# The product with v of a window of rows: all six pairs of heads in one run of matmuls

## The chip, the cores and the metric

The kernel runs on one core of one Trainium2 chip. The metric is device time in microseconds (us), as the median of the runs of one kernel. Engines are named as in the profile: PE is TensorE (PEld its weight loads), DVE VectorE, ACT ScalarE, POOL GpSimd, SP the engine that issues the DMAs.

## The reference

Attention that mixes its heads twice, then two feed-forward blocks. B, H, S, D = 2, 12, 448, 64; the blocks have 896 tokens of 768, with 1536 and 2048 inner columns. All is float32; the weights of the blocks are float64 on input.

```
scores = einsum('bhij,hg->bgij', q @ k.T / sqrt(D), w_pre)
attn   = exp(scores - max(scores)); attn = attn / (sum(attn) + 1e-9)
x      = einsum('bhij,hg->bgij', attn, w_post) @ v      # tokens x 768
xn     = x / sqrt(mean(x * x) + 1e-6) * rms_g
x2     = (silu(xn @ w_gate) * (xn @ w_val)) @ w_out
out    = elu(x2 @ w_in) @ w_out2
```

## The kernel before

The kernel has an attention stage, up to about 293 us, and then products with the weights. The change lies in the attention, so this section keeps to it.

**Scores and groups.** For each batch and head, q and k are transposed on PE (`k_turn`, `q_turn`), multiplied in chunks of 112 rows (`scores`, L407 and L408), copied by ACT (L418) and stored to device memory with (row, head) order (L419). They come back two groups at a time (`load_group`, L440). A group is ten rows, each with its twelve heads: 120 partitions. A batch has 45 groups, the last of eight rows. A group goes through: split into two parts on ACT and POOL (L468, L469; every other group takes the unsplit float32), premix on PE (L476, or L479 to L481), maximum on DVE (L488), exponential on ACT (L496), reciprocal (L511), high and low float16 parts (L524 or L526, and L533), postmix on PE with twelve small matmuls (L554), and a copy by ACT into the tile `at` (L566), which then holds key position on the partitions and (chunk, head, row) along them.

**Windows.** `at` collects the groups of a window: six or seven groups, 48 to 70 rows, seven windows a batch, fourteen in all (`WGS`, L539). When a window's last group is in, `window(b, w)` puts pieces of work into the queue `wq`: the product with v, `av(kk)` for pair kk of heads. One `av` is 16 records on PE (four chunks, two heads, two passes of float32), 64 columns each, the two heads on the two halves of the partitions of one PSUM tile `psv_t` (L590). The last of these pieces also puts the list `chain` into the queue `cq`: squares (DVE L596, then POOL L603 to L606, or ACT L601 for the last two windows), nothing, mean (PE L612), root (DVE, POOL L623), nothing, diagonal (DVE L627), spread (PE L631), normed (DVE L634), high (ACT L640) and low (DVE L643), one piece a step. They leave the normed tokens in `xh` and `xl`. The last window of the first batch then also issues the loads of the second batch's v (L314).

**The order of the work** is written out by hand, in a loop over steps t (from L749). The engines take their instructions in the order in which they are issued. Step t issues, by engine:

- ACT: copies that follow the last step's matmuls; the copy to `at` of group t - 4; split of group t + 3; exponential of group t; high part of group t - 1
- DVE: sum of t - 1, maximum of t, reciprocal of t - 1, low part of t - 2, then what follows the last step's transposes
- PE: premix of t + 1, postmix of t - 3, then 1.4 to 1.5 pieces of scores or transposes a step (later pieces that convert weights, on ACT and DVE), then one piece of each chain in `cq`, then one piece of `wq` (two from t = 90 on)

Premix, scores, transposes, mean and spread share five PSUM buffers (`psa`, L66); a buffer comes free when ACT or DVE has read it. The postmix has two of its own, `psv_t` one, `at` two.

At the end of the attention `first_gate` gives twelve triples of matmuls of the gated block (L197 to L199), which need only the first batch's tokens; `fill` puts them between the last pieces, one a step.

```
        for _ in range(2 if t >= n else 1):
            if wq:
                wq.pop(0)()
        ...
    for _ in range(GAP):
        step_chains()
        fill(1)
    while wq:
        wq.pop(0)()
    while cq:
        step_chains()
        fill(END)
```

Of the kernel before, what the change touches and what calls it, by code (L numbers as in the profile page):

```python
# [21 lines left out]
def block_kernel(  # L22
# [32 lines left out]
    SIGN = -0x80000000  # L55
    # a float64's upper word read as a float32, times REBASE: its exponent three bits
    # to the right of a float32's; F32_MAX is then the largest float32
    REBASE = 2.0**-112
# [12 lines left out]
    def split(h, l, x, h_eng="act"):  # L71
        """x = h + l, each part exact in float32r."""
        if h_eng == "act":
            nc.scalar.activation(out=h, in_=x, func=ACTF.Copy)
        else:
            nc.vector.tensor_copy(out=h, in_=x)
        nc.vector.tensor_tensor(out=l, in0=x, in1=h.bitcast(F32), op=ALU.subtract)

    ctx.enter_context(tc.manual_schedule())

# [1 line left out]
    ident = const.tile([P, P], F32, name="ident")  # L82
# [6 lines left out]
    nc.vector.memset(mhalf, -0.5)  # L89
    # w_pre and w_post once per row of a group, on the diagonal blocks  # L90
    setup = wpool.tile([P, KD * P], F32, tag="w32", name="setup", bufs=1)
# [30 lines left out]
    def mixing():  # L122
        """Pieces that make the matrices that mix the heads."""
        selr, cmax, rcm, m2p = slot(H, GI, H), slot(P, H), slot(P, H), slot(GP, H, GI)
        a1 = m1.rearrange("p i g -> p (i g)")
        a2 = m2.rearrange("p i g -> p (i g)")
        rep = {}

        def select():
            nc.vector.tensor_copy(out=selr, in_=ident[:H, :H].unsqueeze(1).to_broadcast([H, GI, H]))  # L130
            nc.vector.tensor_reduce(
                out=cmax, in_=wpb.rearrange("p (h g) -> p g h", h=H), axis=AXX, op=ALU.max,
                apply_absolute_value=True,
            )
            nc.vector.tensor_scalar_max(cmax, cmax, 1e-30)

        def repeat():
            rep[0] = ps_a()
            nc.tensor.matmul(
                out=rep[0][:GP, :2 * H], lhsT=selr.rearrange("p i h -> p (i h)"),  # L140
                rhs=wpp.rearrange("p t h -> p (t h)"), start=True, stop=True,
            )
            nc.vector.reciprocal(out=rcm, in_=cmax)

        def copies():
            for t, m in enumerate((m1, m2)):
                nc.vector.tensor_copy(
                    out=m, in_=rep[0][:GP, t * H:(t + 1) * H].unsqueeze(1).to_broadcast([GP, GI, H])
                )

        def blocks():
            for m in (m1, m2):
                nc.gpsimd.affine_select(
                    out=m, in_=m, pattern=[[-H, GI], [0, H]], compare_op=ALU.is_ge, fill=0.0, base=0,
                    channel_multiplier=1,
                )
                nc.gpsimd.affine_select(
                    out=m, in_=m, pattern=[[H, GI], [0, H]], compare_op=ALU.is_ge, fill=0.0, base=H - 1,
                    channel_multiplier=-1,
                )  # L160
            # what the postmix leaves to be multiplied, for head 2 k + half on the partitions' halves
            for s in range(2):
                nc.vector.tensor_scalar_mul(
                    vsc[s * D:(s + 1) * D], cmax.rearrange("p (k s) -> p s k", s=2)[s * D:(s + 1) * D, s], BACK
                )

        def pre():
            # premix matrix, with the scores' scale
            nc.vector.tensor_scalar_mul(a1, a1, 1.0 / float(D) ** 0.5)
            nc.vector.tensor_copy(out=m1f, in_=a1)  # L170
            nc.vector.tensor_copy(out=m1h, in_=a1)
            nc.vector.tensor_tensor(out=m1l, in0=a1, in1=m1h.bitcast(F32), op=ALU.subtract)

        def post():
            # postmix matrix: columns of w_post over their maximum, in (head, row) order
            nc.vector.tensor_tensor(
                out=m2, in0=m2, in1=rcm[:GP].unsqueeze(1).to_broadcast([GP, GI, H]), op=ALU.mult
            )
            nc.vector.tensor_scalar_mul(m2p, m2.rearrange("p i g -> p g i"), W_UP)
            nc.vector.tensor_copy(out=m2h, in_=m2p)  # L180
            nc.vector.tensor_tensor(out=m2l, in0=m2p, in1=m2h, op=ALU.subtract)

        return [select, repeat, copies, blocks, None, pre, post]

    # normed tokens, later the first block's output: [d, token]
    xh = xpool.tile([P, KD, NT], F32R, tag="xh", name="xh")
# [3 lines left out]

# [1 line left out]
    HALF = [slice(b * S, (b + 1) * S) for b in range(B)]  # L192

    def gemm(ps, wh, wl, xh_, xl_, nk, first=True, last=True):
        """ps = w.T @ x in three passes of split operands."""
        for kk in range(nk):
            nc.tensor.matmul(out=ps, lhsT=wh(kk), rhs=xh_(kk), start=(first and kk == 0), stop=False)  # L197
            nc.tensor.matmul(out=ps, lhsT=wh(kk), rhs=xl_(kk), start=False, stop=False)  # L198
            nc.tensor.matmul(out=ps, lhsT=wl(kk), rhs=xh_(kk), start=False, stop=(last and kk == nk - 1))  # L199
# [9 lines left out]
    def convert(u):  # L209
        """Pieces that turn a block of float64 weights into float32r parts h + l."""  # L210
        raw, (_, _, nk, nf, scale) = raws[u], units[u]
# [50 lines left out]

    # the weights' blocks in the order of their use, loaded and converted ahead of it
    NH = DM // 2
    units = []
# [7 lines left out]
    raws, ready, begun = [], {}, [0]  # L273
# [14 lines left out]
    def first_gate(j):  # L288
        """The first columns of gate or val for the first batch, a matmul triple at a time."""
        hf = HALF[0]  # L290
# [12 lines left out]
    def attention(actx):  # L303
# [14 lines left out]
        def load_qk(b, h):  # L318
            """q, and k twice side by side."""
            qt = ap.tile([CP, NCH, D], F32, tag="qt", name="qt", bufs=2)  # L320
# [6 lines left out]
        def load_first():  # L327
            """The first heads' q and k at once, in room that is not yet in use."""
            n_at = NCH * H * WMAX
# [22 lines left out]
        def parts_of(b, h):  # L352
            """Room for a head's parts, some of it where the weights will be."""
            if (b, h) not in par:
# [11 lines left out]
        def q_split(b, h):  # L366
            # both parts side by side, so that they come out one above the other
            qt, _ = qk_sb[b, h]
# [5 lines left out]
        def k_turn(b, h):  # L374
            # twice, under both parts of q
            _, kt = qk_sb.pop((b, h))
# [44 lines left out]

        # what follows from the matmuls of the last step
        on_act, on_dve = [], []
# [5 lines left out]

# [1 line left out]
        LG = 2  # L431
# [24 lines left out]
        def whole(b, g):  # L456
            """Groups whose premix takes float32 as it is; the others' takes parts."""
            i = b * NG + g
            return i % WHOLE == 1 and not PARTS[0] <= i < PARTS[1]
# [77 lines left out]

        # windows of groups, for the product with v
        WGS = [[0, 7, 14, 21, 27, 33, 39, NG], [0, 7, 14, 21, 28, 34, 40, NG]]  # L539
# [30 lines left out]
        def window(b, w):  # L570
            """The work after a window's last group, in pieces."""
            t0 = WGS[b][w] * GI
# [85 lines left out]

            return [lambda k0=k0, k1=k1: some(k0, k1) for k0, k1 in ((0, 2), (2, 3), (3, 4), (4, 5), (5, 6))]

# [1 line left out]
        heads = [(b, h) for b in range(B) for h in range(H)]  # L662
        EARLY, FAST, RATE, LATE = 4, 1.5, 1.4, 1.4

        def turn(i):
            """Pieces that leave head i ready for its products."""

# [68 lines left out]
        conv_now = []  # L736
        # the last groups' tail runs beside the next product's first matmuls
        gates = []
# [75 lines left out]
    def run(u, mm, stages):  # L814
        """A unit's matmuls, with the later units' conversion and the earlier one's outputs beside them."""
        load_to(u + 4)
# [13 lines left out]

# [1 line left out]
    uh = big.tile([P, KF, NT], F32R, tag="bh", name="uh", padded_shape=[P, KF2, NT])  # L832
# [71 lines left out]

# [1 line left out]
    gh = big.tile([P, KF2, NT], F32R, tag="bh", name="gh")  # L906
    gl = big.tile([P, KF2, NT], F32R, tag="bl", name="gl")

    def elu(pss, fc):
        # max(-relu(1 - exp(h)), h)  # L910
        t = {}
# [24 lines left out]

# [1 line left out]
    NTT = NT // P  # L938
# [71 lines left out]
```

## Time and profile before

| | |
|---|---|
| median of 3 runs | 788.56 us (787.6 to 790.57) |
| span of the profiled execution, which is the time that the page gives for it | 787.3 us |
| busy in the span: PE, DVE, ACT, POOL | 759.4, 550.6, 445.6, 114.4 us |
| mean granted PE clock | 0.990 |
| product with v (L590), all of it | 1344 records, 55.7 us busy |

The span runs from the first to the last instruction of one profiled execution; the median is 1.3 us longer. Matmuls overlap, so their times are best read from start to start. "Idle before <-releaser" in a row is the time that the engine stood still before the instruction, and what ended it. The granted clock is a share of 2.4 GHz.

### The profile page before, as it was taken

The numbers are of one execution on the slowest core, as the hardware profiler recorded it, in microseconds if no ns is written. First come the engines' busy times: TensorE is split into PE (matmuls) and PEld (weight loads), VectorE is DVE, ScalarE is ACT, GpSimd is POOL, SyncE is SP. The second block draws the span as 40 slices with busy tenths as digits, with TensorE's granted clock in tenths as the row PEclk, the third lists the DMA queues.
The fourth block names the chain that finished last, engine by engine and source line by source line (L and its number), as shares of the span: only waits on it lengthen the run. The fifth ranks groups of instructions, "written<-read, shape, count | busy, mean of one in ns | idle before, by whom it ended". The sixth has DMA issues, their size and how long they took to land.

```text
span 787.3 us, 14708 instructions
## 1 busy us (share of the span) xinstructions
PE 759.4 (96%) x5655; PEld 673.1 (85%) x5655; DVE 550.6 (70%) x1135; ACT 445.6 (57%) x952; POOL 114.4 (15%) x141
## 2 busy tenths in 40 slices
PE   6779999999998999999999999999999999999997
PEld 5557778777776779999999999999999999999997
DVE  6356999665789938887877865652898887553651
ACT  7679888887987925654544433231576566221320
POOL 4212565333443400000000000000000000000000
PEclk9899999999998999999999999999999999999999
DMA  7798665668783303343332333231444343433512
GB/s 205 222 280 252 168 154 140 178 173 236 217 230 78 104 2 121 122 132 108 121 112 94 116 121 106 95 121 41 121 132 120 109 122 100 111 111 111 155 47 70
DMA packets 90249, 105.42 MB, mean 134 GB/s; under 512 B 16004, under 2 KB 86084, under 8 KB 90180
## 3 DMA queue, kind: packets, MB, share of 16 engines
q1 hardware_dynamic: 90180, 104.49, 46.0%
q8 instruction: 44, 0.72, 0.4%
q14 instruction: 25, 0.20, 0.1%
HBM read 82.46 MB, written 22.02 MB: 133 GB/s over the span
## 4 chain that ended last, share of the span: by engine, by line
PE 83%; DVE 7%; DMA 5%; ACT 2%; issue 1%; SPq 1%; POOL 1%; ACTq 0%; POOLq 0%
PE psa_t L197 13%; PE psa_t L198 13%; PE psa_t L199 13%; PE psv_t L590 5%; PE pst_t L554 4%; PE psf_t L198 4%; PE psf_t L199 4%; PE psf_t L197 4%; PE psa_t L966 3%; PE psa_t L964 3%; PE psa_t L965 3%; DMA s_d<-st 3%; PE psa_t L476 3%; DMA sg<-s_d 2%; PE psa_t L407 2%; DVE el L533 1%
## 5 line engine op out<-in xcount | busy, mean ns | idle before, releaser
L554 PEld LDWEIGHTS <-eh 120*112 120x112 f16 x720 | 66.8, 131 | 27.2 <-issue 21.8
L240 ACT ACTIVATE whl<-w 128x768 fp32r<-128x768 f32 x44 | 37.1, 844 | 86.0 <-PE psf_t L966 28.5
L244 ACT ACTIVATE whl<-w,g_sb 128x128 fp32r<-128x128 f32 x144 | 45.0, 393 | 64.1 <-PE psa_t L199 25.6
L219 ACT ACTIVATE w<-raw 128x768 f32<-128x768 f32 x68 | 62.5, 919 | 30.5 <-DVE whl L251 23.6
L469 POOL TENSOR_TENSOR sl<-sg,sh 120x448 fp32r<-120x448 f32 (+1 forms) x45 | 54.5, 1211 | 116.2 <-ACT sh L468 111.6
L251 DVE TENSOR_TENSOR whl<-w,whl 128x768 fp32r<-128x768 f32 x44 | 42.2, 958 | 41.1 <-ACT whl L240 40.0
L198 PE MATMUL psa_t<-x2l,whl 128*128 128x448 f32 x192 | 70.1, 365 | 0.0
L199 PE MATMUL psa_t<-x2h,whl 128*128 128x448 f32 x192 | 70.1, 365 | 0.0
L197 PE MATMUL psa_t<-x2h,whl 128*128 128x448 f32 x192 | 70.1, 365 | 0.0
L233 DVE SCALAR_TENSOR_TENSOR w<-w,raw 128x768 int32<-128x768 int32 x68 | 65.2, 958 | 2.3
L554 PE MATMUL pst_t<-m2h,eh 120*112 120x120 f16 x360 | 63.0, 217 | 2.7 <-ACT at L566 2.6
L227 DVE SCALAR_TENSOR_TENSOR raw<-raw 128x768 int32<-128x768 int32 x68 | 64.8, 953 | 0.0
L554 PE MATMUL pst_t<-m2h,el 120*112 120x120 f16 x360 | 63.1, 218 | 1.7 <-DVE el L533 1.7
L496 ACT ACTIVATE e<-psa_t,nmax 120x448 f32<-120x448 f32 (+1 forms) x90 | 58.0, 645 | 11.4 <-DVE rs L511 10.4
L533 DVE SCALAR_TENSOR_TENSOR el<-e,rs,eh 120x448 f16<-120x448 f32 (+1 forms) x90 | 64.0, 711 | 0.3 <-ACT eh L524 0.3
L554 PE MATMUL pst_t<-m2l,eh 120*112 120x120 f16 x360 | 63.0, 218 | 0.0
L488 DVE TENSOR_REDUCE nmax<-psa_t 120x1 f32<-120x448 f32 (+1 forms) x90 | 55.2, 613 | 8.4 <-PE psa_t L481 8.3
L197 PE MATMUL psa_t<-xh,whl 128*128 128x448 f32 x150 | 55.7, 372 | 1.0 <-ACT xh L640 1.0
L590 PE MATMUL psv_t<-at,vs 112*64 112x70 f32 (+3 forms) x1344 | 55.7, 230 | 0.0
L590 PEld LDWEIGHTS psv_t<-at,vs 112*64 112x64 f32 x1344 | 46.5, 139 | 9.9 <-issue 7.0
L198 PE MATMUL psa_t<-xl,whl 128*128 128x448 f32 x150 | 54.9, 366 | 0.0
L199 PE MATMUL psa_t<-xh,whl 128*128 128x448 f32 x150 | 54.8, 365 | 0.0
(167 smaller groups left out, 2059.2 us busy)
## 6 DMA issues: line engine op xcount, KB each, us to landing
raw<-in_moe_w_out_dram SPq DMA_DIRECT2D x28, 768.0 KB, 4.5
sg<-s_d SPq DMA_DIRECT2D x44, 420.0 KB, 5.0
s_d<-st SPq DMA_DIRECT2D x93, 196.0 KB, 3.2
raw<-in_moe_w_in_dram SPq DMA_DIRECT2D x16, 768.0 KB, 4.7
raw<-in_moe_w_gate_dram SPq DMA_DIRECT2D x12, 768.0 KB, 4.3
raw<-in_moe_w_val_dram SPq DMA_DIRECT2D x12, 768.0 KB, 4.4
vs<-in_v_dram SPq DMA_DIRECT2D x4, 672.0 KB, 7.7
kt<-in_k_dram SPq DMA_DIRECT2D x12, 224.0 KB, 3.8
```

Of the source, the lines that this page charges most:

```text
L197: nc.tensor.matmul(out=ps, lhsT=wh(kk), rhs=xh_(kk), start=(first and kk == 0), stop=False)
L198: nc.tensor.matmul(out=ps, lhsT=wh(kk), rhs=xl_(kk), start=False, stop=False)
L199: nc.tensor.matmul(out=ps, lhsT=wl(kk), rhs=xh_(kk), start=False, stop=(last and kk == nk - 1))
L219: nc.scalar.activation(out=w, in_=raw.bitcast(F32)[:, :, 1], func=ACTF.Copy, scale=REBASE)
L227: nc.vector.scalar_tensor_tensor(out=lo, in0=hi, scalar=SIGN, in1=lo, op0=ALU.bitwise_and, op1=ALU.bitwise_or)
L233: nc.vector.scalar_tensor_tensor(out=wi, in0=wi, scalar=3, in1=lo, op0=ALU.logical_shift_left, op1=ALU.bitwise_or)
L469: nc.gpsimd.tensor_tensor(out=sl[:r], in0=s32, in1=sh[:r].bitcast(F32), op=ALU.subtract)
L488: nc.vector.tensor_reduce(out=nmax[:r], in_=ps[:r, :S], axis=AXX, op=ALU.max, negate=True)
L496: nc.scalar.activation(out=e32[:r], in_=ps[:r, :S], func=ACTF.Exp, bias=nmax[:r], scale=1.0, accum_out=sm[:r])
L533: nc.vector.scalar_tensor_tensor(out=el[:r], in0=e32[:r], scalar=rs[:r], in1=eh[:r], op0=ALU.mult, op1=ALU.subtract)
L554: nc.tensor.matmul(out=o, lhsT=lhs[:r, c * CP:(c + 1) * CP], rhs=rhs[:r, :, :ni], start=(n == 0), stop=(n == 2),)
L590: nc.tensor.matmul(out=psx[s * D:(s + 1) * D, kk, :n], lhsT=vs[b][:, hh, c, :], rhs=at[:, c, hh, :n], start=(c == 0), stop=(c == NCH - 1),)
```

## The change

`window` returns one piece, which calls `av` for all six pairs and puts the chain into `cq`, in place of five pieces (two pairs, then one pair four times). The matmuls and their operands are the same, and so are the chain's pieces; the whole product is issued in the step in which its first piece was issued before, and the chain begins one step later. Otherwise the diff only blanks comments, line by line, so that line numbers stay.

```diff
             def some(k0, k1):
                 for kk in range(k0, k1):
                     av(kk)
                 if k1 == KD:
                     cq.append(chain)
                     if w == NW - 1 and b + 1 < B:
                         load_v(b + 1, 0)
                         load_v(b + 1, 1)
 
-            return [lambda k0=k0, k1=k1: some(k0, k1) for k0, k1 in ((0, 2), (2, 3), (3, 4), (4, 5), (5, 6))]
+            return [lambda k0=k0, k1=k1: some(k0, k1) for k0, k1 in ((0, 6),)]
```

## Rows read from the trace of the kernel before

**Rows 1.** The page: busy time by engine, and the chain's shares by engine
```profile
PE 759.4 (96%) x5655; PEld 673.1 (85%) x5655; DVE 550.6 (70%) x1135; ACT 445.6 (57%) x952; POOL 114.4 (15%) x141
...
PE 83%; DVE 7%; DMA 5%; ACT 2%; issue 1%; SPq 1%; POOL 1%; ACTq 0%; POOLq 0%
```

**Rows 2.** Chain of waits, 60 to 296 us: start us, us, engine, tile, line
```profile
105.95 0.54 DVE par L386
...
185.81 8.91 DMA s_d<-st
...
196.41 0.63 PE pst_t L554 x12
...
225.99 0.53 DVE nmax L488
...
264.49 0.59 DVE el L533
```

**Rows 3.** Busy us by stretch: from:to length, PE PEld DVE ACT POOL, PEclk, DMA, GB/s
```profile
60.00:70.00 10.00, 9.94 (x103) 7.28 (x104) 7.11 (x21) 10.00 (x26) 2.67 (x3) 1.00 0.87 268
160.00:170.00 10.00, 10.00 (x118) 7.38 (x116) 7.19 (x23) 8.91 (x23) 4.24 (x6) 1.00 0.72 208
210.00:220.00 10.00, 10.00 (x137) 7.64 (x135) 6.31 (x20) 9.05 (x23) 2.83 (x3) 1.00 0.73 207
240.00:250.00 10.00, 8.03 (x73) 6.26 (x71) 9.87 (x26) 7.25 (x19) 4.85 (x7) 0.66 0.18 45
...
246.00:248.00 2.00, 2.00 (x23) 1.46 (x20) 2.00 (x7) 1.19 (x3) 0.61 (x1) 0.50 0.00 0
```

**Rows 4.** Timeline of PE around runs: start us, us, engine, line, what
```profile
146.87 0.37 PE L408 MATMUL psa_t<-par_r 128*112 128x448 f32 x1
...
147.83 0.21 PE L554 MATMUL pst_t<-m2h,eh 120*112 120x120 f16 x1
...
155.16 0.36 PE L408 MATMUL psa_t<-par 128*112 128x448 f32 x1
155.45 1.15 PE L590 MATMUL psv_t<-at,vs 112*64 112x60 f32 x32
...
157.38 0.22 PE L554 MATMUL pst_t<-m2h,eh 120*112 120x120 f16 x1
...
161.25 0.37 PE L408 MATMUL psa_t<-par 128*112 128x448 f32 x1
...
163.01 0.22 PE L554 MATMUL pst_t<-m2h,eh 120*112 120x120 f16 x1
...
172.34 1.15 PE L590 MATMUL psv_t<-at,vs 112*64 112x58 f32 x32
...
210.00 1.19 PE L590 MATMUL psv_t<-at,vs 112*64 112x70 f32 x32
...
226.84 1.19 PE L590 MATMUL psv_t<-at,vs 112*64 112x70 f32 x32
```

**Rows 5.** Timeline of ACT, 202 to 207 us
```profile
202.04 0.67 ACT L566 ACTIVATE at<-pst_t 112x480 f32<-112x480 f32 x1
...
204.09 0.69 ACT L566 ACTIVATE at<-pst_t 112x480 f32<-112x480 f32 x1
...
206.12 0.55 ACT L418 ACTIVATE st<-psa_t 112x448 f32<-112x448 f32 x1 [0.26 <-PE psa_t L408]
206.56 0.57 ACT L566 ACTIVATE at<-pst_t 112x480 f32<-112x480 f32 x1
```

**Rows 6.** Timeline of PE and DVE, 243 to 252 us
```profile
243.52 0.35 PE L554 MATMUL pst_t<-m2h,el 120*112 120x120 f16 x1 [1.08 <-DVE el L533]
...
245.06 2.13 PE L590 MATMUL psv_t<-at,vs 112*64 112x70 f32 x32
...
251.90 0.15 DVE L504 TENSOR_SCALAR sm<-sm 120x1 f32<-120x1 f32 x1 [0.32 <-ACT e L496]
```

**Rows 7.** Timeline of PE at the end of the attention
```profile
293.63 0.47 PE L197 MATMUL psa_t<-xh,whl 128*128 128x448 f32 x1 [1.02 <-ACT xh L640]
```

## The prediction

> **What bounds the kernel now.** Start with the page: TensorE is busy for 96% of the span, and 83% of the chain that ended last is its work [rows 1]. That is a mean over three stages, and the change touches only the attention, up to about 293 us, so the second view is the chain of waits in order of time [rows 2]. There it lies on TensorE for most of the stretch from 65 to 293 us, but not all of it. For ten us up to 106, and from 226 to 264.5 us, it runs through VectorE instructions, and at 185.8 us there are 8.9 us of score stores. The third view, the busy times by stretch [rows 3], says how near the next engine is. ScalarE is busy 10.00 of 10 us at 60 to 70 us and 9.05 at 210 to 220, beside a TensorE at 9.94 and 10.00; at 240 to 250 us VectorE has 9.87 and TensorE only 8.03. So where scores are still made (to about 225 us) TensorE sets the pace with ScalarE close behind, and later VectorE sets it.
>
> **What one run costs.** I read the boundaries of a run from TensorE's timeline [rows 4]. From a score's last matmul to the first postmix matmul, with a premix between, it is 147.83 - 146.87 = 0.96 us with no run in between, 163.01 - 161.25 = 1.76 us with a run of one pair (16 records), and 157.38 - 155.16 = 2.22 us with two pairs (32). So a run of one pair costs 0.80 us of TensorE, but a pair that is appended to a run costs only 0.46. A removed run gives back 0.34; I take 0.32, as an entry behind a postmix costs a little less. Runs removed: twelve windows go from five to one (48); the last but one goes from three to one and the last from two to one, since the pieces are then taken two a step (3). That makes 51, and 51 x 0.32 = 16.3 us of TensorE's time at most.
>
> A rule of the Trainium skill bears on this. TensorEngine Tiling (Array Packing), Key Properties, says that changing the tiling mode drains TensorE, and these 64-column matmuls on two halves of the array are such a mode. The 0.34 us agree with it. By that rule alone all 16 us would come off; whether they do depends on the other engines, and is the first rival.
>
> **What the burst does to the others.** The six pairs are now one run of 1.15 + 4 x 0.46 = 3.0 us at the end of one step, and the six other steps of a window have none. Behind it on TensorE wait the next group's premix (0.85 us) [rows 4], a postmix (0.63) [rows 2] and the step's scores. TensorE can't have worked ahead: psa has five buffers, a step takes about 2.4 of them (a premix and 1.4 scores), and the premix's is held until the exponential of its group. So TensorE and ScalarE are at the same step, and when the run begins ScalarE has the rest of its step and one more in stock, 2.3 to 3.2 us. That covers the run. But ScalarE's step after that begins with copies of scores that TensorE makes only after premix and postmix, 0.85 + 0.63 and a score, about 2 us later: an idle of some 2.0 us per window.
>
> ScalarE's own work follows from its copies to at [rows 5]: 204.09 - 202.04 = 2.05 us for one step, 206.56 - 204.09 - 0.26 of waiting = 2.21 for the next, with two scores in the pair of steps; with 1.4 a step (0.45 us for each more) 2.3 us a step. Six steps and one high part (0.5) are 14.3 us, with the new idle 16.3. A six-group window now takes 172.34 - 155.45 = 16.9 us [rows 4], so by this count 0.6 us is saved there, not 4 x 0.32 = 1.28. For seven groups: 16.6 + 2.0 = 18.6 us against 226.84 - 210.00 = 16.8 now, but that window's last two steps have no scores, and ScalarE's waits for the last score of a step that holds a run, as the 0.26 us at 206.12 [rows 5], go. Bounds for one window of the score stretch: a gain of 1.28 (all kept) to a loss of 0.9 (2.0 of new idle and 0.2 of delay less 1.28, nothing recovered). I take a gain of 0.3, half of what the six-group rows give because the seven-group count points the other way, for each of the six windows from 122 to 210 us: 1.8 us. For the first window (67 us) I take nothing, as ScalarE there has 10.00 of 10.
>
> **The windows that VectorE sets.** At 85, 107, 227, 245 and 260 us I take nothing. Saved TensorE time becomes idle there, and the burst is absorbed. The rows nearest to it [rows 6]: at 245.06 us a run of two pairs took 2.13 us at a granted clock of 0.50 (1.2 GHz) [rows 3], with premix and postmix as slow behind it, and VectorE lost 0.32 us (251.90). Bounds: 0.6 us either way in each, as VectorE's own steps of the chain of pieces (squares, normed, low) move four steps earlier and meet other conversions.
>
> **The end.** From 265 us TensorE drains what is left with the others falling idle. Two runs of the last but one window and one of the last go: 3 x 0.32 = 1.0 us. The wait that follows, 1.02 us before the first product that needs the last window [rows 7], stays: the twelve matmul triples set aside to fill are as many as before, they run out before the spread, and behind it come normed, high and low as now.
>
> **What moves at no cost.** The chain of pieces starts four steps earlier, with the same instructions on each engine. Its period still is one window, so normed of one window still meets squares of the next. The loads of the second batch's v are issued four steps earlier on SP's queue, where they wait for the first batch's last run, and two stores and a load of groups queue behind them; they are 1.3 MB beside the stores, and today's 8.91 us of a store [rows 2] stands right behind them. TensorE loses little in it now. I take no difference, with 0.6 us of gain to 2 us of loss as bounds. The buffers of at and psv come free earlier, and nobody waits for them.
>
> **Sum.** 1.8 + 1.0 = 2.8 us off the profiled span of 787.3, so 784.5; the median of the runs lies 1.3 above that span, so 788.56 - 2.8 = 785.8 us. A measurement of this kernel can tell about 0.5% (3.9 us) from no change.
>
> **Rivals.** First: the saving is kept wherever the chain is on TensorE today. That leaves out the windows at 85, 227, 245 and 260 us (16 runs): 35 x 0.32 = 11.2 us, 777.4 us; with all 51, 772. For it: TensorE's 10.00 of 10 over long stretches. Against it: ScalarE at 9 to 10 of 10 beside it and the five buffers. Chance 0.28.
>
> Second, slower: the burst starves ScalarE. Place: the step but one after each run, in the score stretch. Price: the 2.2 us of idle and delay less the 1.28 saved, 0.9 us a window, in all seven score windows, 6.3 us: 794.9 us. It decides where ScalarE has no room to catch up, which is when six or seven of its steps and 2.2 us are longer than the window's period now: so at 67 and at 210 us by the numbers above, and elsewhere if its copies also wait for stores. For it: 10.00 of 10 at 60 to 70 us. Against: 8.91 of 10 at 160 to 170 us [rows 3]. Chance 0.16.
>
> Third, also slower: the clock. At 242 to 243.5 us TensorE sat waiting (1.08 us before the row at 243.52), and the granted clock was 0.50 behind it [rows 3, 6]; a run of two pairs then took 2.13 instead of 1.19 us [rows 4, 6]. Had the new pauses behind a burst that effect, a run of six pairs would cost about 2.8 us more, three of them 8.5: 797 us. The Trainium skill, TensorE: Matmul & The Clock Gate, Part 1, says that the throttled state is the default and that activity releases it; the trace agrees at this one place. Against it: the new pauses are ScalarE's, and TensorE's own lie under 1 us. Chance 0.04.
>
> **Numbers.** The forecast has 0.52, of which 0.46 lie within 0.5%, 0.04 below and 0.02 above. Faster by over 0.5%: 0.28 + 0.04 = 0.32. Slower: 0.16 + 0.04 + 0.02 = 0.22. The range goes three quarters of the way to the first rival and to the second, 779.5 to 792.5; the forecast's own is 782 to 789.
>
> **What would show it.** Right: 14 runs of 96 records (48 pairs of passes) of 3.0 us each in the timeline; an idle of ScalarE of about 2 us before a copy of a score, once per window, one step after the run; the period of the six-group windows within 0.6 us of now; the stretch from 226 to 264 us as long as now with more idle on TensorE; 1.0 us less from the last exponential to the first product of the gated block; that product's wait still 1.0 us. Wrong: windows between 122 and 210 us shorter by over 1 us (first rival), longer than now (second), or granted clocks of 0.50 behind the runs (third).

## The result and the profile after

The changed kernel takes 796.6 us (median of four runs, 795.57 to 806.54) where the kernel before, run beside it, takes 789.57: a ratio of 1.0111, with a 95% interval of 1.007 to 1.0151. The ratios, here and below, leave out the executions that took over 1.5% longer than the fastest of their kernel; the medians count all. The forecast was 785.8 us, and its range ended at 792.5. The profiled execution has a span of 795.2 us, 7.9 more than before. The page after has less TensorE work than before, and less of the chain on TensorE [rows 1]: what was added is waiting.

The page, busy time by engine and the chain's shares:

```profile
PE 752.3 (95%) x5655; PEld 672.9 (85%) x5655; DVE 548.4 (69%) x1135; ACT 442.9 (56%) x952; POOL 109.4 (14%) x141
...
PE 78%; DVE 8%; DMA 7%; ACT 5%; issue 2%; SPq 1%; ACTq 0%; DVEq 0%
```

Busy times by stretch (the columns of [rows 3]):

```profile
160.00:170.00 10.00, 10.00 (x88) 7.85 (x87) 7.18 (x20) 8.93 (x24) 4.89 (x7) 1.00 0.60 179
180.00:190.00 10.00, 4.06 (x33) 3.01 (x31) 2.80 (x9) 3.75 (x10) 0.00 (x0) 0.87 0.76 203
190.00:200.00 10.00, 10.00 (x117) 7.83 (x117) 6.66 (x20) 9.14 (x23) 3.02 (x4) 0.79 0.80 235
210.00:220.00 10.00, 10.00 (x157) 8.53 (x156) 7.32 (x22) 9.25 (x23) 2.62 (x4) 1.00 0.77 216
240.00:250.00 10.00, 6.22 (x60) 4.40 (x58) 8.70 (x21) 8.11 (x22) 3.15 (x3) 1.00 0.41 113
```

Where scores are made, 160 to 170 and 210 to 220 us look as they did. One stretch stands out: from 180 to 190 us TensorE is busy for 4.06 of 10 us, ScalarE for 3.75, while the DMA engines are busy for 0.76 of it. To see what that costs, take the start of each window's product from TensorE's timeline and compare the distances (us, from the profiled executions; the third kernel is an experiment below):

| from the start of window's run | before | after | e1_v_load_late |
|---|---|---|---|
| 1 to 7 (after: 66.55 to 171.82) | 105.1 | 105.3 | 103.7 |
| 7 to 8 (171.82 to 198.05) | 18.3 | 26.2 | 17.6 |
| 8 to 10 (to 233.29) | 36.2 | 35.2 | 36.7 |
| 10 to 12 (to 269.43) | 33.3 | 36.1 | 33.1 |
| 12 to the first product that waits for the last window (to 301.50) | 33.5 | 32.1 | 32.8 |
| sum | 226.4 | 234.9 | 223.8 |

The step from the seventh window to the eighth has 7.9 us of loss, nearly all of it; the other rows add up to 0.6, with 2.8 more from the tenth window to the twelfth and less elsewhere. That step is where the first batch ends and the second batch's v is loaded. The chain of waits of the changed kernel, 165 to 205 us, shows what TensorE waited for (start us, us, what):

```profile
171.89 1.59 PE psv_t L590 x49
173.48 2.03 issue
...
177.86 7.12 DMA s_d<-st
185.05 4.31 DMA sg<-s_d
189.50 1.82 PE psa_t L476 x2
...
198.12 3.07 PE psv_t L590 x96
```

A score store that takes 7.12 us, then a load of groups, then the premix. SP's timeline says why that store was late. Before (start us, us, queue, line, what, count):

```profile
174.73 0.30 SPq L419 DMA_DIRECT2D s_d<-st  x1
177.02 0.83 SPq L440 DMA_DIRECT2D sg<-s_d  x2
178.74 3.36 SPq L419 DMA_DIRECT2D s_d<-st  x3
184.23 0.90 SPq L314 DMA_DIRECT2D vs<-in_v_dram  x2
```

After:

```profile
171.08 0.30 SPq L419 DMA_DIRECT2D s_d<-st  x1
174.87 1.86 SPq L314 DMA_DIRECT2D vs<-in_v_dram  x2
176.83 1.41 SPq L419 DMA_DIRECT2D s_d<-st  x3
185.05 0.83 SPq L440 DMA_DIRECT2D sg<-s_d  x2
```

Four steps earlier means ahead of the last three stores of a chunk, and so ahead of the two group loads that may be issued only when all twelve heads of that chunk are stored. The pair of loads comes at 185.05 instead of 177.02 us, 8.0 us later. ScalarE's timeline of the changed kernel gives the first part:

```profile
175.51 0.54 ACT L418 ACTIVATE st<-psa_t 112x448 f32<-112x448 f32 x1 [2.04 <-issue]
...
184.11 1.02 ACT L418 ACTIVATE st<-psa_t 112x448 f32<-112x448 f32 x2 [2.40 <-DMA s_d<-st]
...
189.45 0.58 ACT L468 ACTIVATE sh<-sg 120x448 fp32r<-120x448 f32 x1 [3.85 <-DMA sg<-s_d]
```

The copy for the last store ends at 176.05 (175.51 + 0.54); before, the store went out at 174.73, as soon as its copy was done: 1.3 us, the new idle behind the run. The store then goes out at 177.86: 1.8 us of waiting on SP, behind two loads that themselves waited for the run and took 1.86 us to issue. The group loads follow that store by 7.2 us, where 2.3 (177.02 - 174.73) did before: 4.9 us, in which the store shares the DMA engines with 1.3 MB of v. Together 8.0. (The seventh run began 0.5 us earlier here; counted from its start the delay is about 8.5 us.) TensorE's timeline shows what arrives:

```profile
171.82 3.01 PE L590 MATMUL psv_t<-at,vs 112*64 112x58 f32 x96
184.71 0.46 PE L407 MATMUL psa_t<-par 128*112 128x448 f32 x1 [1.81 <-ACT st L418]
189.50 1.82 PE L476 MATMUL psa_t<-sg,m1f 120*120 120x448 f32 x2 [4.13 <-DMA sg<-s_d]
252.31 4.76 PE L590 MATMUL psv_t<-at,vs 112*64 112x70 f32 x96
301.50 0.48 PE L197 MATMUL psa_t<-xh,whl 128*128 128x448 f32 x1 [1.02 <-ACT xh L640]
```

It stands still for 1.81 + 4.13 = 5.9 us, and what follows runs at half clock until 194 us, as the granted clocks by two us say (the premix at 189.50 us took 1.82 us there; those at whole clock take 0.92 to 1.01):

```profile
186.00:188.00 2.00, 0.00 (x0) 0.00 (x0) 0.00 (x0) 0.00 (x0) 0.00 (x0) 0.87 0.90 213
188.00:190.00 2.00, 0.50 (x1) 0.47 (x2) 0.00 (x0) 0.55 (x2) 0.00 (x0) 0.50 1.07 230
...
192.00:194.00 2.00, 2.00 (x11) 1.73 (x10) 1.80 (x7) 1.27 (x4) 0.00 (x0) 0.50 0.99 263
```

The chain's 4.6 us of work from 189.5 would have taken about half, which gives the other 2 us of the 7.9.

### The profile page after: what moved, and what is told of

It is laid out like the page before. It is cut to its first block, busy times and chain, and to the rows that moved or that the text cites. A ratio compares the mean times of both kernels' runs of the same rounds, so it can differ in the third digit from the quotient of the medians.

```text
span 795.2 us, 14712 instructions
## 1 busy us (share of the span) xinstructions
PE 752.3 (95%) x5655; PEld 672.9 (85%) x5655; DVE 548.4 (69%) x1135; ACT 442.9 (56%) x952; POOL 109.4 (14%) x141
## 4 chain that ended last, share of the span: by engine, by line
PE 78%; DVE 8%; DMA 7%; ACT 5%; issue 2%; SPq 1%; ACTq 0%; DVEq 0%
PE psa_t L197 13%; PE psa_t L198 12%; PE psa_t L199 12%; PE psv_t L590 5%; PE psf_t L199 4%; PE psf_t L197 4%; PE psf_t L198 4%; PE psa_t L964 3%; PE psa_t L965 3%; PE psa_t L966 3%; PE pst_t L554 3%; DMA s_d<-st 3%; DMA sg<-s_d 3%; PE psa_t L476 2%; DVE el L533 2%; DVE nmax L488 2%
## 5 line engine op out<-in xcount | busy, mean ns | idle before, releaser
L469 POOL TENSOR_TENSOR sl<-sg,sh 120x448 fp32r<-120x448 f32 (+1 forms) x45 | 52.3, 1163 | 116.8 <-ACT sh L468 112.7
L566 ACT ACTIVATE at<-pst_t 112x480 f32<-112x480 f32 (+1 forms) x90 | 53.5, 594 | 8.9 <-PE pst_t L554 8.9
L418 ACT ACTIVATE st<-psa_t 112x448 f32<-112x448 f32 x81 | 42.7, 562 | 19.8 <-PE psa_t L408 9.1
```

The source lines that it names most:

```text
L469: nc.gpsimd.tensor_tensor(out=sl[:r], in0=s32, in1=sh[:r].bitcast(F32), op=ALU.subtract)
L566: nc.scalar.activation(out=at_of[b, w][:, :, :, i0:i0 + ni], in_=pt.pop((b, g))[:CP, :, :, :ni], func=ACTF.Copy)
```

## The experiments

Three theories were set against each other. Theory 1: the place of the v loads on SP's queue costs, and the merged run itself does not. Theory 2: the run of six at the seventh window costs there by itself. Theory 3: every run costs a little. All ratios are to the kernel before, run on the same chip, with a 95% interval.

**e1_v_load_late.** Merged runs and early chain as changed; the v loads four steps later.

```diff
-                    if w == NW - 1 and b + 1 < B:
-                        load_v(b + 1, 0)
-                        load_v(b + 1, 1)
-            return [lambda k0=k0, k1=k1: some(k0, k1) for k0, k1 in ((0, 6),)]
+            def next_v():
+                if w == NW - 1 and b + 1 < B:
+                    load_v(b + 1, 0)
+                    load_v(b + 1, 1)
+            return [lambda: some(0, 6)] + [lambda: None] * 3 + [next_v]
```

> All windows in one run as in the changed kernel, but the loads of the second batch's v are issued four steps later, where the kernel before has them: on SP's queue behind three stores of scores and two loads of groups instead of ahead of them. Theory 1 (the loss is the place of these loads, 1.3 MB ahead of the stores that the next groups wait for): the 4.1 us wait of the premix for its group goes, and 6 to 6.5 us of the loss: about 790 us against 796.6 of the changed kernel and 789.6 before. Theory 2 (the loss is the long run of the seventh window itself, which makes scores and their stores late): stays near 796. Theory 3 (many small losses behind all runs, and the half clock): 794 to 796.

Measured: 787.33 us, ratio 0.9983 [0.9954, 1.0012]. The loss is gone. SP's timeline has the group loads ahead of the v loads again:

```profile
177.32 0.83 SPq L440 DMA_DIRECT2D sg<-s_d  x2
178.38 3.27 SPq L419 DMA_DIRECT2D s_d<-st  x3
181.69 1.07 SPq L314 DMA_DIRECT2D vs<-in_v_dram  x2
```

The run of six is still there (170.51 us, 96 records, 3.01 us), so theory 2 falls.

**e2_only_w7.** The kernel before, with only the seventh window in one run (the v loads move with it).

```diff
+            runs = ((0, 6),) if b == 0 and w == NW - 1 else ((0, 2), (2, 3), (3, 4), (4, 5), (5, 6))
```

> The kernel before, with only the seventh window of the first batch in one run; its loads of v come four steps earlier with it, the thirteen other windows keep their runs. Theory 1: almost the whole loss, about 6 us over before (795.5 to 796). Theory 2: the same. Theory 3: one fourteenth of it, within 1 us of before (789 to 790.5).

Measured: 798.31 us, 1.0115 [1.0081, 1.0149]: this one window has the whole loss, a little over the 795.5 to 796 expected. Its chain has the same two pieces:

```profile
176.32 6.96 DMA s_d<-st
...
183.35 4.29 DMA sg<-s_d
```

**e3_all_but_w7.** The changed kernel with only the seventh window in five runs.

```diff
+            runs = ((0, 6),) if b or w < NW - 1 else ((0, 2), (2, 3), (3, 4), (4, 5), (5, 6))
```

> The changed kernel, with only the seventh window of the first batch back in five runs. Theories 1 and 2: 6 to 6.5 us faster than the changed kernel, about 790. Theory 3: 796. If the merged runs of the thirteen others bring the 2.8 us of the prediction, 787.

Measured: 788.42 us, 0.9985 [0.9965, 1.0005]. Thirteen merged windows cost nothing that can be measured, so theory 3 falls too.

**e5_run_alone.** Only the matmuls are merged; chain and v loads stay at the step of the last of the five old pieces.

```diff
+            def rest():
+                cq.append(chain)
+                if w == NW - 1 and b + 1 < B:
+                    load_v(b + 1, 0)
+                    load_v(b + 1, 1)
+            return [lambda: some(0, 6)] + [lambda: None] * 3 + [rest]
```

> The six pairs in one run, and nothing else moved: the pieces squares to low and the loads of v stay at the steps of the kernel before (four steps after the run). By the theory that the run itself gains a little and the place of the loads made the loss: 786.5 to 788.5, as the kernel with only the loads put back (787.3). If the earlier pieces squares to low are what gained there (or lost), it differs from that one by more than 1.5 us.

Measured: 788.62 us, 1.0000 [0.9974, 1.0027], at the upper end of what was expected. Its ratio is not told apart from that of e1, which has the early chain, so the chain's place is not what costs.

**e4_v_on_pool.** The changed kernel, with the second batch's v loads issued by GpSimd at the same early step: the bytes, without the wait on SP.

```diff
-            nc.sync.dma_start(out=vs[b][:, hs], in_=...)
+            (nc.gpsimd if b else nc.sync).dma_start(out=vs[b][:, hs], in_=...)
```

> The changed kernel, with the loads of the second batch's v issued by GpSimd instead of SP, at the same step: they start as early, but no store waits behind them on SP's queue. If what costs is the place on SP's queue (stores issued only after the wait for the long run and behind the loads): about 790. If what costs is that the transfer itself shares the DMA engines with the stores at that time: still 794 to 796, with store times of 7 us as in the changed kernel.

Measured: 791.63 us, 1.0024 [0.9997, 1.0051], between the two that were expected, and not told apart from no change; the twelve executions lie between 786.5 and 799.1 us, and the traced one, at 795.4, is among the slower. The last store now goes out at once (its copy ends at 177.80 us), as the timeline of SP and GpSimd shows (lines are one higher here):

```profile
174.82 3.31 SPq L420 DMA_DIRECT2D s_d<-st  x3
176.91 1.75 POOL L314 DMA_DIRECT2D vs<-in_v_dram  x2 [1.94 <-PE psv_t L591]
...
183.28 0.83 SPq L441 DMA_DIRECT2D sg<-s_d  x2
```

Yet the group loads follow it only 5.4 us later (the last of the three is issued in the last 0.30 us of the row, from 174.82 + 3.31 - 0.30 = 177.83, and they come at 183.28), where it was 2.3 before. The Trainium skill, DMA: Bandwidth & Descriptors, Issuing engines are not separate DMA queues, says that DMAs of all issuing engines run on the same sixteen DMA engines, and that another issuer saves no more than the time of issuing. The 5.4 us agree with the first. The second does not come out here, by one trace of each: the stretch from the seventh run to the eighth takes 21.9 us (195.44 - 173.57), 4.3 less than in the changed kernel, where issuing the two loads took SP 1.86 us.

**e12_wait_alone.** The counterpart: the wait without the bytes. At the early place one head of v is loaded, the other eleven at the old place.

```diff
+            if half == 2 or (half == 0 and not skip):
...
+            hs = slice(half * H // 2 + skip, (half + 1) * H // 2) if half < 2 else slice(0, 1)
...
-                        load_v(b + 1, 0)
-                        load_v(b + 1, 1)
+                        load_v(b + 1, 2)
+            def next_v():
+                if w == NW - 1 and b + 1 < B:
+                    load_v(b + 1, 0, 1)
+                    load_v(b + 1, 1)
+            return [lambda: some(0, 6)] + [lambda: None] * 3 + [next_v]
```

> The wait on SP's queue without the bytes: at the early place only one head of the second batch's v is loaded (112 KB, in place of 1344), and it waits for the first batch's last run as the whole did; the other eleven heads come at the old place. In the changed kernel the pair of group loads is issued 8.0 us later than before: the last score's copy ends 1.3 us later, the store then stands 1.8 us behind the waiting loads and their issue, and lands 4.9 us later than the store before did. If the wait is what costs: the group loads come at 183 to 185 us on SP's queue, the premix waits 2 us or more, 793 to 797 us. If the bytes ahead of the store cost: the last store lands in 2 to 3.5 us, the group loads are issued at 179 to 181.5, the premix waits under 1.5 us, and from the seventh window's start to the eighth's it takes 17.5 to 20 us: 787 to 790 us.

Measured: 790.96 us, 1.0029 [1.001, 1.0048]; 19.2 us from the seventh run to the eighth. The chain in this kernel:

```profile
176.06 2.53 DMA s_d<-st
178.73 4.28 DMA sg<-s_d
```

The store stands 1.6 us on the queue (its copy ends at 174.49) but lands in 2.53, and the premix waits 1.35 us instead of 4.13. These are, nearly to the number, the signs that were set for the bytes, though the time lies just above their range. The wait alone costs some 0.3%, the bytes alone (e4) 0.2% with an interval that takes in no change, and both together 1.1%, more than the two added. That the two delays lie one behind the other on one chain, whose slack is there only once, would explain it; this is argued, not shown.

**e8_v_between.** The changed kernel, but the v loads issued in the loop over steps, behind the three stores and ahead of both group loads.

```diff
-                    if w == NW - 1 and b + 1 < B:
-                        load_v(b + 1, 0)
-                        load_v(b + 1, 1)
...
+                if t == 50:
+                    load_v(1, 0)
+                    load_v(1, 1)
                 load_group(b, g)
```

> The changed kernel with the loads of v one place later on SP's queue: behind the three stores, still ahead of the two loads of groups. If the loss is two transfers one after the other (stores behind v, 7.1 us, and then the groups' load that waits for them, 4.3 us), the stores now land in time and only the load of groups is late: 790 to 793. If any place ahead of the groups costs the same: 796. If only the stores matter: 787 to 788.

Measured: 792.38 us, 1.0053 [1.0032, 1.0074]; 23.0 us from the seventh run to the eighth. Now the store is quick and the group load is slow:

```profile
175.04 2.23 DMA s_d<-st
177.34 8.48 DMA sg<-s_d
```

8.48 us instead of 4.31. The bytes cost whichever of the two they stand ahead of.

**e7_three_three.** Two runs of three pairs.

```diff
-            ... for k0, k1 in ((0, 6),)]
+            ... for k0, k1 in ((0, 3), (3, 6))]
```

> Two runs of three pairs in two steps. The loads of v come three steps earlier than before, but in SP's order they stand where they stood, behind three stores and two loads of groups, because those are issued at the step between. If the order on the queue decides: 787 to 789. If the time of the loads decides: 792 or more.

Measured: 791.95 us, 1.0028 [1.0001, 1.0054]. The expectation was wrong on the queue: the v loads stand between the two group loads here (177.11 a group load, 177.55 the v loads, 178.53 the other), not behind both. So it belongs to the series of places, below, though it differs from the others in its runs too.

**e9_v_halves.** As e1, with the second half of v one step later still.

```diff
-            return [lambda: some(0, 6)] + [lambda: None] * 3 + [next_v]
+            return [lambda: some(0, 6)] + [lambda: None] * 3 + [lambda: next_v(0), lambda: next_v(1)]
```

> One run, the loads of v at the old place, and the second half of them one step later still, behind another load of groups. In the kernel with the loads put back ScalarE still waited 3.2 us for a store behind v and the chain of waits had a store of 8.0 us there; if that costs, 1 to 2 us less than there: 785.5 to 786.5. If TensorE covers it, no difference (787.3).

Measured: 793.32 us, 1.0071 [1.0041, 1.01]. A miss: too late costs too. The eighth window's product waits for v, and half clock follows; the chain and TensorE's timeline:

```profile
184.51 8.93 DMA vs<-in_v_dram
```

```profile
193.48 3.07 PE L590 MATMUL psv_t<-at,vs 112*64 112x70 f32 x48 [2.56 <-DMA vs<-in_v_dram]
...
248.51 5.87 PE L590 MATMUL psv_t<-at,vs 112*64 112x70 f32 x96
```

Even at the old place there is no room to spare, since a run of six needs all of v at once. In e1 the same product waits for its second half:

```profile
190.79 1.68 PE L590 MATMUL psv_t<-at,vs 112*64 112x70 f32 x48 [1.02 <-DMA vs<-in_v_dram]
```

**e6_run_last.** The run of six moved to the step of the last of the five old pieces.

```diff
-            return [lambda k0=k0, k1=k1: some(k0, k1) for k0, k1 in ((0, 6),)]
+            return [lambda: None] * 4 + [lambda: some(0, 6)]
```

> The run of six moved to the step of the last of the five old pieces, the chain and the v loads with it at their old steps; the order of SP's queue is the one of before. Theory 1: no loss, 787 to 789.5 us, ratio 0.997 to 1.0005, and 17.5 to 19 us from the seventh window's start to the eighth's less the shift of both. A rival, that holding the tile of the finished window four steps longer makes the copies into the next tile but one wait: it would need a wait of ScalarE's copy into that tile for the product, and 1 us or more a window, 14 us, 803; the tile has two buffers and the copies into the second next begin two steps after the run at the earliest, so I expect none.

Measured: 790.69 us, 1.0025 [1.0001, 1.0048], a little over what was expected; 20.4 us from the seventh run to the eighth, in which ScalarE waits 2.5 us for a store. No copy into `at` waits for a product, so the rival named there falls. Why it is behind e5 stays open.

**e11_not_at_half.** As e1, with the two windows that begin near 245 and 260 us left in five runs.

```diff
+            if b == B - 1 and w in (3, 4):
+                return [lambda k0=k0, k1=k1: some(k0, k1) for k0, k1 in ((0, 2), (2, 3), (3, 4), (4, 5), (5, 6))]
```

> One run of six in twelve of the fourteen windows, the loads of the second batch's v four steps after the last run of the first batch (their old place behind the score stores and group loads), and the two windows that begin near 245 and 260 us left in five runs. Theory 1 (only the place of the v loads costs; merging itself gives back what TensorE saves in the score stretch and at the end, 2 to 3 us): 786 to 787.5 us, ratio 0.996 to 0.998. With the second part of it, that a run of 96 records in a half-clock stretch costs up to 2 us more than one of 32: 1 to 2 us below the kernel that merges all fourteen (787.3), so 786, and no run of 96 records longer than 3.2 us in the trace. Theory 3 (merging costs a little in every window): 788.5 to 790, no better than before.

Measured: 788.71 us, 0.9998 [0.997, 1.0027], no better than e1, and in the range that was set for theory 3; its interval takes in theory 1's ratio of 0.998 as well, so it decides nothing between them. That keeping these windows apart brings anything is not shown. Its traced execution (795.94 us) lost its time behind the attention: 501.1 us (793.9 - 292.84) from the first product that waits for the last window to the end, where before has 493.7 (787.3 - 293.63). No version was found that beats the kernel before by more than can be measured.

The places of the v loads on SP's queue, in order: ahead of the three stores 1.0111 [1.007, 1.0151]; behind them and ahead of both group loads 1.0053 [1.0032, 1.0074]; between the group loads, with two runs of three, 1.0028 [1.0001, 1.0054]; behind both, with all runs merged, 0.9983 [0.9954, 1.0012] (e1), 1.0000 [0.9974, 1.0027] (e5) and 1.0025 [1.0001, 1.0048] (e6); later still 1.0071 [1.0041, 1.01]. The two places ahead of both group loads are the dear ones, which supports theory 1; the place between them is not told apart from e6. How the price divides into the wait and the bytes is not shown by the medians. By one trace of each, the stretch from the seventh run to the eighth takes 18.3 us before, 19.2 with the wait alone (e12), 21.9 with the bytes alone (e4) and 26.2 with both, which puts more on the bytes.

## Why the prediction was wrong

- **The step that failed** is the v loads in "What moves at no cost", taken as no difference with 2 us of loss as the bound. The text had the move and the wait; of what queues behind, it counted two stores and one load of groups, where the trace has three stores and two loads. It did not ask who waits for those: it looked at TensorE in the trace of before, where the v loads stood behind both group loads. The 8.91 us store [rows 2] behind them held up a copy of ScalarE there, but TensorE only for 0.56 us (timelines of ScalarE and of TensorE before):

```profile
194.80 0.54 ACT L418 ACTIVATE st<-psa_t 112x448 f32<-112x448 f32 x1 [3.33 <-DMA s_d<-st]
...
195.40 1.01 PE L476 MATMUL psa_t<-sg,m1f 120*120 120x448 f32 x2 [0.56 <-ACT st L418]
```

  In the new place the same bytes stand ahead of a store that a group load waits for, and that load ahead of a premix. Measured: 7.9 us in that stretch. The group loads came 8.0 us later, 1.3 from ScalarE's idle, 1.8 from the queue, 4.9 while the store shared the DMA engines with v; slack took some of it, and the half clock behind the idle gave as much back. That 796.6 us lies near the 794.9 and 797 of the second and third rivals is chance: neither has this step.
- **The run** was right: 3.01 to 3.14 us where the clock is whole, against 3.0.
- **ScalarE's idle** came about as large as predicted: 0.94 to 2.81 us before a copy of a score, in each of the six windows in which scores follow the run (1 and 5 to 9), against "some 2.0". In five of them it comes behind premix, postmix and score, as the text has it. The 2.04 us of the seventh window, nearest to the number, are another wait: there the score comes directly behind the run, and ScalarE's stock did not cover the run, so that this agreement is luck. ScalarE's timeline, and the end of that score on TensorE:

```profile
161.00 0.98 ACT L418 ACTIVATE st<-psa_t 112x448 f32<-112x448 f32 x2 [0.94 <-PE psa_t L408]
...
203.10 0.98 ACT L418 ACTIVATE st<-psa_t 112x448 f32<-112x448 f32 x2 [2.81 <-PE psa_t L408]
```

```profile
175.05 0.37 PE L408 MATMUL psa_t<-par_r 128*112 128x448 f32 x1
```

- **The second rival** is out as a whole, but not where it was said to decide. The three windows of six groups took 48.2 us (123.64 to 171.82), before 49.9 (122.42 to 172.34), a gain of 0.6 each, where 0.3 was taken. The windows that begin near 67 and 210 us, which the rival names, are longer: 18.8 us (66.55 to 85.35) against 18.2 (67.23 to 85.46), and 17.4 (215.94 to 233.29) against 16.8 (210.00 to 226.84), 0.6 and 0.5 of the 0.9 it priced.
- **The end** was right: 32.1 us from the twelfth run on, 1.4 less than before (0.7 less in e1), where 1.0 was taken, and the wait is 1.02 us as before [rows 7].
- **The sum without the failed step**, 2.8 us off, agrees with e1's profiled execution (784.3 us against 787.3), one of the faster of its twelve, and lies inside its interval by medians: 789.2 - 787.33 = 1.9 us, of which the interval leaves 1.0 of loss to 3.6 of gain. So a gain at all is not shown, and the windows made it up otherwise than the text did: three of them brought 0.6 each, and the one at 210 us lost. A gain of all 11 or 16 us, the first rival, is excluded by e1, e3 and e5: what TensorE saves is for the most part lost again in waits (in e1 it is busy 748.3 us in place of 759.4, and idle 36.0 in place of 27.9; some of the busy time of before is its half clock, and the waits are not told apart).
- **The third rival's mechanism** came, but by another door. From 186 to 188 us the clock fell while TensorE waited for DMA, not behind a burst's pauses, and later the run of six at 252 us took 4.76 us at a granted clock of 0.57 to 0.58 (252 to 256 us). Windows 10 to 12 are 2.8 us longer in the changed kernel's profile, of which 1.6 are this run, and the clock was 0.50 again from 266 to 268 us; in e1 and e8 they are not. The trace of before has a clock of 0.50 at 246 to 248 us too [rows 3], so it takes no merged run. Each kernel left one trace, and whether this goes by the kernel or by the execution is not shown.
- **Left open:** the third window (105.58 to 123.64 us) took 18.1 us in the changed kernel, e3 and e11, 16.5 in e1 and e8, and 15.6 before and in e5: 2.5 us of loss in the changed kernel, which the gains of other windows cover. The text took nothing there. No experiment separates what does that.

## What to carry to other kernels

When a change moves a DMA, list the queue's order around its old and its new place, and follow each transfer that it now stands ahead of to the instruction that needs it: a load that waits for a buffer holds up everything behind it on its queue, and once issued it shares the DMA engines with what follows, even with other queues' transfers. What a transfer costs at its old place says nothing about a new one. When work is merged and a side effect hangs on its last piece, decide on the side effect's place by itself.

## What the runs showed of the hardware

A run of six in a stretch of half clock loses in one piece what a run of two pairs loses in part (0.94 us, 2.13 against 1.19 [rows 4, 6]). Two kernels' timelines around 245 us, both with all runs merged, e5 (clock 0.55 from 243 to 249 us) and e1 (1.00 from 243 to 246 us):

```profile
243.54 5.43 PE L590 MATMUL psv_t<-at,vs 112*64 112x70 f32 x96
```

```profile
243.03 3.14 PE L590 MATMUL psv_t<-at,vs 112*64 112x70 f32 x96
```

The run of 96 records took 3.14 us at full clock and 4.76 to 5.87 us, 1.6 to 2.7 more, in the traces where the clock had fallen. Whether it falls there differs between kernels that are alike in that stretch; what decides it is not shown.
